# Strassen's scheme for the first feed-forward layer of the last six blocks

## The chip, the cores and the metric

The kernel runs on one core of a Trainium2 chip. The metric is the device time of one execution in microseconds (us), from launch to end, lower being better. A core has a matrix engine (TensorE, PE in the rows, with its weight loads listed apart as PEld), a vector engine (DVE), a scalar engine (ACT), a general engine (GpSimd, POOL), and a queue engine (SyncE, SP) that only issues DMAs. Each engine works through its own list of instructions in order and waits at semaphores for the others.

## The reference, cut to what matters

```python
def _moe_ref(x, w_ch1, w_ch2):
    X = np.fft.fft(x, axis=1)
    X = np.fft.fft(X, axis=2)
    u = x + np.real(X)
    mu = np.mean(u, axis=-1, keepdims=True)
    var = np.mean((u - mu) ** 2, axis=-1, keepdims=True)
    un = (u - mu) / np.sqrt(var + 1e-06)
    ch = np.maximum(un @ w_ch1, 0.0) @ w_ch2     # 512 -> 2048 -> 512
    return u + ch
```

`x` is the output of two attentions over 8 batches of 576 tokens (a pooled one and one in a band), 4608 tokens of 512 channels in all. Everything is float32.

## The kernel before

**Stages.** The first 330 us hold the attention, the Fourier mixing (as matrix products) and the decoding of the weights, which arrive as 64-bit numbers in quarters (class `Quarter`: fetch, size, clamp, join, high, low). The rest is the feed-forward part: nine blocks of 512 tokens (class `Block`, `NBLK` = 9, numbered 0 to 8).

**Three products for one.** The matrix engine multiplies in a rounded 32-bit format (`F32R`). To keep float32's precision each factor is held as a high part `h` and a low part `l`, and a product is taken as h·h + l·h + h·l. So w1 lies in SBUF as `wts[f, 1]` (two tiles of 128 x 4 x 128 per f, for the 16 groups f of 128 hidden channels), w2 as `wts[f, 2]`, and the transposed normalised tokens as `unT` (one such pair of 128 x 4 x 512 for even blocks and one for odd ones).

**One block.** For each f, `first` (line 958) issues 12 matmuls, 3 parts by 4 chunks of the 512 channels, each with 128 x 128 weights and 512 columns, into one PSUM bank `hps`. `high` (ACT, line 962) applies the ReLU into `hh`, `low` (DVE, line 966) makes `hl`, the rest. `second` (lines 976 to 978) issues 12 more matmuls of 512 columns that add the group's share into four accumulator banks `acc`. At the end of a block `finish` (DVE, line 982) adds the input `u`, `store` (line 986) writes it out. Meanwhile the next block's four tiles of 128 tokens are loaded (lines 900 to 906; the latter two kinds are adding DMAs issued by POOL), normalised (`stats`, `norm`), transposed on the matrix engine (`turn`, line 932: 4 matmuls into a bank `tpn`) and split (`turn_high` on ACT, `turn_low` on DVE). Four PSUM banks are `acc`; the other four are handed out by `bank`.

**Order of the work.** It is written out by hand: `at(fn, t=...)` files an event, and after the events placed by the table `TURNS` all others are issued in order of `t`. The unit `ITEM` (1.6) stands for 12 matmuls of 512 columns on the matrix engine, so an f takes 2 `ITEM` and a block 51.2 units. `second(f)` stands one `ITEM` after `first(f + 1)` has begun.

**Places in memory.** `raws` (four tiles of 128 x 512) and `joins` (four of 128 x 256) serve the decoding of the weights and are idle after it. `wts[f, 1]` is used by every block. Its tiles for f = 0 to 2 lie in the pool `res`, 3 and 4 in `pt`, 5 to 8 in `middle`, 9 to 15 in `more`.

Of the kernel before, what the change touches and what calls it, by code (L numbers as in the profile page):

```python
# [8 lines left out]
F32 = mybir.dt.float32  # L9
F32R = mybir.dt.float32r  # L10
# [3 lines left out]
ALU = mybir.AluOpType  # L14
# [10 lines left out]
ITEM = 1.6  # L25
# [220 lines left out]
def kernel(  # L246
# [13 lines left out]
    nc = tc.nc  # L260
    P = 128
# [4 lines left out]
    NCC = DM // P  # L266
    NF = DFF // P
# [107 lines left out]
    p1, plocal, pseq, pmix = (ExitStack() for _ in range(4))  # L375
# [3 lines left out]
    p2 = plocal.enter_context(tc.tile_pool(name="p2", bufs=2, side="right"))  # L379
# [36 lines left out]
    class Pooled:  # L416
# [258 lines left out]
    class Mix:  # L675
# [203 lines left out]
    out_rows = out.rearrange("b s c -> (b s) c")  # L879

    class Block:


        def __init__(self, n):
            self.n = n
            self.st, self.un, self.tp = {}, {}, {}
# [101 lines left out]
        def plan(self, t, f0, f1):  # L988

            for f in range(f0, f1):  # L990
                at(self.first, f, t=t)
# [42 lines left out]

    def close_d():
        pmix.close()
        weight_tiles(pool("more"), range(*CHUNKS[2:]))

    for close in (close_b, close_a, close_e, close_d):
        at(close)  # L1040
# [6 lines left out]
    t = 0.0  # L1047
    starts = {}
    for n, f0, f1 in [(0, 0, ROUND), (1, 0, ROUND), (0, ROUND, NF)] + [(n, ROUND * (n == 1), NF) for n in range(1, NBLK)]:
        starts[n] = t  # L1050
        t = blocks[n].plan(t, f0, f1)
        if f1 == NF and 0 < n < NBLK - 1:
            for i in range(TILES):
                for part in range(3):
                    at(blocks[n + 1].load, i, part, t=starts[n] + 6 + 0.5 * i + 2.5 * part)
                blocks[n + 1].prepare(i, starts[n] + 12 + i * (t - starts[n] - 18) / TILES)


    for x in quarters:
# [142 lines left out]
```

## Time and profile before

| | us |
|---|---|
| three runs | 1150.66, 1151.46, 1159.52 |
| their median | 1151.46 |
| the profiled execution | 1145.82 |
| its span, first to last instruction | 1144.0 |

The profiled execution was 5.6 us shorter than the median of the runs. Times in the rows are from its span's start. A matmul's busy time in the rows includes its way through the array and overlaps the next one's, so the rate of the matrix engine is read from the starts of successive rows, not from the mean of one.

### The profile page before, as it was taken

The page shows a single profiled execution, that of the slowest core. Times are in us where ns is not written, and L with a number is a line of the kernel's source. Part 1 is how long each engine was busy: PE and PEld are TensorE (multiplying, and loading weights), DVE is VectorE, ACT ScalarE, POOL GpSimd, SP SyncE. Part 2 cuts the span into 40 slices and gives each one's busy share as a digit, 9 for nine tenths or more (in the row PEclk, how much of TensorE's full clock was granted, in tenths as well). Part 3 has the DMA queues.
Part 4 walks back from the last instruction along what each step waited for, and adds up shares of the span by engine and source line. Part 5 has one row for each costly group of instructions (what it writes and reads, how often), then busy time and mean ns, then how long its engine had stood idle before and what let it go on. Part 6 is the DMA issues. An engine that isn't in the chain of part 4 may idle for free.

```text
span 1144.0 us, 20389 instructions
## 1 busy us (share of the span) xinstructions
PE 1108.0 (97%) x8172; PEld 935.8 (82%) x8172; DVE 545.4 (48%) x1226; ACT 358.4 (31%) x1050; POOL 293.5 (26%) x411
## 2 busy tenths in 40 slices
PE   7899999899889999999999999999999999999998
PEld 6788888889778788888888888888888888888886
DVE  4889999899878776322212222222222222222111
ACT  4777767767544443111111111111111111111110
POOL 2444545355574553203002002001101100200000
PEclk7999999999999999999999999999999999999999
DMA  8888777777685332506006005105103302400000
GB/s 257 269 257 252 215 240 247 234 217 181 181 188 161 109 123 93 110 1 148 1 1 147 1 1 129 19 1 121 27 1 95 53 1 71 77 1 37 1 1 37
DMA packets 57901, 123.07 MB, mean 108 GB/s; under 512 B 7280, under 2 KB 7408, under 8 KB 57552
## 3 DMA queue, kind: packets, MB, share of 16 engines
q1 hardware_dynamic: 44288, 92.23, 24.6%
q0 software_dynamic: 13520, 29.55, 14.7%
q8 instruction: 64, 1.05, 0.4%
q14 instruction: 29, 0.24, 0.1%
HBM read 89.88 MB, written 30.74 MB: 105 GB/s over the span
## 4 chain that ended last, share of the span: by engine, by line
PE 79%; DVE 10%; DMA 6%; issue 2%; SPq 1%; ACT 1%; POOL 0%; DVEq 0%; ACTq 0%; POOLq 0%
PE hps L958 34%; PE acc L976 11%; PE acc L978 11%; PE acc L977 11%; DMA vsum<-in_vg_dram 3%; PE y L744 2%; PE av L625 1%; PE avd L483 1%; PE sc L566 1%; PE tpn L932 1%; DVE sums L552 1%; DMA raw<-in_wq_dram 1%; PE mix L789 1%; DVE xeo L710 1%; DVE w L697 1%
## 5 line engine op out<-in xcount | busy, mean ns | idle before, releaser
L966 DVE SCALAR_TENSOR_TENSOR hl<-hps,hh 128x512 fp32r<-128x512 f32 x144 | 99.1, 690 | 456.3 <-ACT hh L962 456.3
L958 PE MATMUL hps<-unT,w1h 128*128 128x512 f32 x1152 | 309.9, 392 | 0.0
L962 ACT ACTIVATE hh<-hps 128x512 fp32r<-128x512 f32 x144 | 86.0, 598 | 539.2 <-PE hps L958 533.9
L958 PEld LDWEIGHTS hps<-unT,w1h 128*128 128x128 f32 x1152 | 215.5, 188 | 45.7
L976 PE MATMUL acc<-w2h,hh 128*128 128x512 f32 x576 | 227.3, 395 | 0.2 <-ACT hh L962 0.2
L978 PE MATMUL acc<-w2h,hl 128*128 128x512 f32 x576 | 225.5, 392 | 0.0
L977 PE MATMUL acc<-w2l,hh 128*128 128x512 f32 x576 | 225.4, 391 | 0.0
L958 PE MATMUL hps<-unT,w1l 128*128 128x512 f32 x576 | 155.2, 392 | 0.0
L978 PEld LDWEIGHTS acc<-w2h,hl 128*128 128x128 f32 x576 | 108.3, 188 | 24.0 <-DVE hl L966 0.4
L958 PEld LDWEIGHTS hps<-unT,w1l 128*128 128x128 f32 x576 | 108.3, 188 | 23.6
L976 PEld LDWEIGHTS acc<-w2h,hh 128*128 128x128 f32 x576 | 108.3, 188 | 23.4 <-ACT hh L962 0.6
L977 PEld LDWEIGHTS acc<-w2l,hh 128*128 128x128 f32 x576 | 108.3, 188 | 22.4
L917 POOL TENSOR_TENSOR rstd<-rstd,mhalf 128x1 f32<-128x1 f32 x36 | 19.9, 554 | 300.3 <-DVE rstd L916 299.1
L902 POOL DMA_DIRECT2D ut<-ux x40 | 35.5, 1002 | 206.7 <-DMA ut<-um 206.3
L584 ACT ACTIVATE sb<-sc,mx 128x64 f32<-128x64 f32 x320 | 69.8, 329 | 2.0 <-PE tpl L596 0.8
L941 DVE TENSOR_TENSOR unT<-tpn,unT 128x512 fp32r<-128x512 f32 x36 | 24.8, 688 | 55.4 <-ACT unT L938 55.4
L552 DVE TENSOR_REDUCE sums<-qkT 128x224 f32<-128x896 f32 (+4 forms) x48 | 44.4, 945 | 11.0 <-DMA qkT<-in_qk_dram 9.2
L566 PEld LDWEIGHTS sc<-qkT 64*64 64x64 f32 x1280 | 46.1, 141 | 3.8 <-DMA qkT<-in_qk_dram 0.6
L625 PE MATMUL av<-vaug,pT 64*64 64x65 f32 x1280 | 47.4, 224 | 1.3 <-DMA vaug<-in_vw_dram 0.7
L724 POOL TENSOR_TENSOR fl<-xeo,fh 128x512 fp32r<-128x512 f32 x32 | 42.0, 1334 | 21.8 <-ACT fh L721 16.3
L625 PEld LDWEIGHTS av<-vaug,pT 64*64 64x64 f32 x1280 | 42.2, 138 | 6.3 <-issue 2.9
L566 PE MATMUL sc<-qkT 64*64 64x64 f32 x1280 | 46.4, 225 | 0.1
(97 smaller groups left out, 1368.1 us busy)
## 6 DMA issues: line engine op xcount, KB each, us to landing
qkT<-in_qk_dram SPq DMA_DIRECT2D x40, 512.0 KB
raw<-in_wq_dram SPq DMA_DIRECT2D x64, 256.0 KB
vaug<-in_vw_dram SPq DMA_DIRECT2D x40, 260.0 KB
out_dram<-ut SPq DMA_DIRECT2D x36, 256.0 KB
um<-o SPq DMA_DIRECT2D x16, 512.0 KB
ut<-ux POOLq DMA_DIRECT2D x32, 256.0 KB, 5.1
ut<-ud POOLq DMA_DIRECT2D x32, 256.0 KB, 5.4
vsum<-in_vg_dram POOLq DMA_DIRECT2D x24, 292.5 KB, 6.7
```

The costliest lines, as they stand in the source:

```text
L552: nc.vector.tensor_reduce(out=to, in_=x[:, :, a - g0 : e - g0], axis=AX.X, op=ALU.add)
L566: nc.tensor.matmul(sc[r, a * W : (a + 1) * W], self.qkT[r, 0, a // 2, o : o + W], self.qkT[r, 1, a // 2, o : o + W], start=False, stop=Tru ...
L584: nc.scalar.activation(out=self.sb[:, a], in_=self.sc[:, a * W : (a + 1) * W], func=AF.Exp, scale=0.125, bias=self.mx[:, a : a + 1],)
L625: nc.tensor.matmul(av[r, a, :], pT[r, 4 * hh + a], va[r, 4 * hh + a, :], start=True, stop=True)
L724: nc.gpsimd.tensor_sub(out=self.fl[:, t], in0=self.x[t], in1=self.fh[:, t].bitcast(F32))
L902: nc.gpsimd.dma_start(out=to, in_=ux[b][k0 : k0 + m, :], accum_op=ALU.add)
L958: nc.tensor.matmul(hps, a[:, c, :], unT[:, x, c, :], start=(i == 0), stop=(i == len(mms) - 1))
L962: nc.scalar.activation(out=hh, in_=self.hps[f], func=AF.Relu)
L966: nc.vector.scalar_tensor_tensor(out=hl, in0=self.hps[f], scalar=0.0, in1=self.hh[f].bitcast(F32), op0=ALU.max, op1=ALU.subtract)
L976: nc.tensor.matmul(acc, hh, w2h, start=start, stop=False)
L977: nc.tensor.matmul(acc, hh, w2l, start=False, stop=False)
L978: nc.tensor.matmul(acc, hl, w2h, start=False, stop=stop)
```

## The change

For blocks 3 to 8 (`FAST` = 3) the product of the first layer is taken two groups f at a time: the 256 hidden channels of a pair j, by 512 channels, by 512 tokens. Each factor is cut into quarters (two halves of the channels by two groups f; two halves of the channels by two halves of 256 tokens), and Strassen's scheme in Winograd's form gives the four quarters of the result from seven products of quarters (p1 = a11·b11, then s2·t2 added onto it; p2 = a12·b21; p3 = s4·b22; p5 = s1·t1; p7 = s3·t3, then a22·t4 added onto it). A product of quarters is 6 matmuls (3 parts by 2 chunks) with 128 x 128 weights and 256 columns. So a pair takes 42 matmuls of 256 columns for 24 of 512. `second` is as it was.

What goes with it:

- `Differences`, once for each of the 8 pairs, in the last part of block 1 and the first of block 2: joins high and low part of w1 again (`rejoin`, DVE), forms t1 to t4 (`differ`, POOL, 4 subtractions), splits them (`high` on ACT, `low` on POOL) and writes the seven quarters and differences to DRAM (`keep`, 14 DMAs of 128 KB a pair on SP).
- `stream`: each pair in each fast block loads its seven pieces of 256 KB back from DRAM on SP, into tiles of `wts[4..10, 1]`, which are no longer needed as such; two sets, by the parity of j.
- For each coming fast block `turn_copy` (ACT) copies the transposed tile, `add_up` (POOL) forms the sums s1 to s4 of quarters, `sum_high` (ACT) and `sum_low` (POOL) split them into `wts[0..3, 1]` (odd blocks) or `wts[12..15, 1]` (even blocks).
- In a fast pair `save` (ACT) copies p1 twice out of PSUM, and `combine` (DVE, six times) adds the products up into two tiles `rows`, from which `high` and `low` now read instead of from PSUM.
- The three banks of a pair are `ab` (p1, p3), `cd` (p2, p5) and `ef` (p7).

```diff
+    STEPS = ("b11", "b21", "t1"), ("t2", "t3"), ("t4", "b22")
...
+        def rejoin(self):
+            for k in range(2):
+                h, l = wts[2 * self.n + k, 1]
+                whole = raws[k].rearrange("p (c f) -> p c f", c=NCC)
+                nc.vector.tensor_add(out=whole, in0=h.bitcast(F32), in1=l.bitcast(F32))
+
+        def differ(self):
...
+            for out, a, b in ((t1, b12, b11), (t2, b22, t1), (t3, b22, b12), (t4, b21, t2)):
+                nc.gpsimd.tensor_sub(out=out, in0=a, in1=b)
...
+        def plan(self, t):
+            at(self.rejoin, t=t)
+            at(self.differ, t=t + 0.5)
+            for i, x in enumerate(parts[3:]):
+                at(self.high, x, t=t + 2.5 + 0.1 * i)
+                at(self.low, x, t=t + 2.55 + 0.1 * i)
+                at(self.keep, x, t=t + 3 + 0.1 * i)
+            for x in parts[:3]:
+                at(self.keep, x, t=t)
...
+            mms = [(y, z, c) for y, z in ((0, 0), (1, 0), (0, 1)) for c in range(2)]
+            for i, (y, z, c) in enumerate(mms):
+                nc.tensor.matmul(
+                    into, w[:, y, c, :], both[z][:, c, :], start=(start and i == 0), stop=(i == len(mms) - 1), skip_group_check=True
+                )
+
+        def open(self, j):
+            ps = [bank("ab"), bank("cd"), bank("ef")]
...
+            self.product(j, self.ps["p1"], "a11", "b11")
+            self.product(j, self.ps["p2"], "a12", "b21")
+            self.product(j, self.ps["p5"], "s1", "t1")
+
+        def more(self, j):
+            self.product(j, self.ps["p1"], "s2", "t2", start=False)
+            self.product(j, self.ps["p7"], "s3", "t3")
+
+        def close(self, j):
+            self.product(j, self.ps["p7"], "a22", "t4", start=False)
+            self.product(j, self.ps["p3"], "s4", "b22")
...
+        def fast_pair(self, j, t):
+
+            f = 2 * j
+            for g, d in enumerate((0.85, 1.35, 2.65)):
+                at(self.stream, j, g, t=t + (d - 8) * ITEM if j > 1 else t + (d - 5) * ITEM)
+            at(self.open, j, t=t)
+            at(self.save, 0, "p1", t=t + 0.5 * ITEM)
+            at(self.more, j, t=t + 0.8 * ITEM)
+            at(self.combine, 11, 0, "p2", t=t + 0.85 * ITEM)
+            at(self.save, 1, "p1", t=t + 1.1 * ITEM)
+            at(self.combine, 2, 1, "p5", t=t + 1.15 * ITEM)
+            at(self.combine, 22, 2, "p7", t=t + 1.3 * ITEM)
+            at(self.close, j, t=t + 2 * ITEM)
+            at(self.combine, 21, 1, "p7", t=t + 2.3 * ITEM)
+            at(self.combine, 12, 2, "p3", t=t + 2.6 * ITEM)
+            for g, d in ((f, 2.45), (f + 1, 3.1)):
+                at(self.hidden, g, t=t + d * ITEM)
+                at(self.high, g, t=t + d * ITEM)
+                at(self.low, g, t=t + (d + 0.05) * ITEM)
+            at(self.second, f, f == 0, False, t=t + 5 * ITEM)
+            at(self.second, f + 1, False, f + 1 == NF - 1, t=t + 7 * ITEM)
...
+            if n + 1 == FAST:
+                for j in range(NF // 2):
+                    Differences(j).plan(starts[n] - 18 + 4 * j)
```

On the matrix engine one f of block 3 stood so before, `first` and the beginning of the other group's `second` (the name after the comma is the weights, the one before it what moves past them):

```order
L958 MATMUL hps<-unT_6051,w1h_6364 128x512 x4
L958 MATMUL hps<-unT_6051,w1l_6365 128x512 x4
L958 MATMUL hps<-unT_6051,w1h_6364 128x512 x4
L976 MATMUL acc<-w2h_6362,hh 128x512 [waits Activation_49]
L977 MATMUL acc<-w2l_6363,hh 128x512
L978 MATMUL acc<-w2h_6362,hl 128x512 [waits DVE_49]
```

In the changed program pair 1 of block 3 begins on the matrix engine with five products (`open` and `more`); names w1h and w1l with numbers are now the places of streamed pieces, to the right of the comma, or of sums, to its left:

```order
L1066 MATMUL ab<-unT_6107,w1l_6117 128x256 x6
L1066 MATMUL cd<-unT_6107,w1h_6120 128x256 x6
L1066 MATMUL cd<-w1h_140,w1h_6412 128x256 x4
L1066 MATMUL cd<-w1l_141,w1h_6412 128x256 x2
L1066 MATMUL ab<-w1h_144,w1l_6413 128x256 x4
L1066 MATMUL ab<-w1l_145,w1l_6413 128x256 x2
L1066 MATMUL ef<-w1h_148,w1h_6416 128x256 x4
L1066 MATMUL ef<-w1l_149,w1h_6416 128x256 x2
L1143 MATMUL acc<-w2h_142,hh 128x512
L1144 MATMUL acc<-w2l_143,hh 128x512
L1145 MATMUL acc<-w2h_142,hl 128x512
```

After the 12 rows of that `second` its `close` follows, on the matrix engine, here with the semaphores that it waits for:

```order
L1066 MATMUL ef<-unT_6107,w1l_6417 128x256 [waits DMAHW1_49,DVE_49]
L1066 MATMUL ef<-unT_6107,w1l_6417 128x256 x5
L1066 MATMUL ab<-w1h_5924,w1l_6121 128x256 [waits DMAHW2_49,Activation_49]
L1066 MATMUL ab<-w1h_5924,w1l_6121 128x256 x3
L1066 MATMUL ab<-w1l_5925,w1l_6121 128x256 x2
```

Where 12 long matmuls with one bank stood, 30 short ones in three banks stand in a row, and then 12 more; each product waits for the DMA of its weights, and those that add onto a bank also for ACT or DVE, which read it.

On ACT the ReLUs of block 2 stood alone before but for a cast of a transposed tile between them:

```order
L962 ACTIVATE hh<-hps 128x512 x2
L938 CAST unT_6051<-tpn 128x4x128
L962 ACTIVATE hh<-hps 128x512 x3
L938 CAST unT_6051<-tpn 128x4x128
L962 ACTIVATE hh<-hps 128x512 x2
```

Now the casts of the differences t1 to t4 (`raw` and `wt` in these rows) stand between the ReLUs on ACT, from block 1's last part on, and wait for POOL:

```order
L923 CAST raw<-raw 128x256 [waits DMAHW7_49,Activation_49,Pool_49]
L923 CAST raw<-raw 128x256 [waits DMAHW1_49,Activation_49,Pool_49]
L923 CAST wt<-wt 128x256 [waits DMAHW3_49,Activation_49,Pool_49]
L923 CAST wt<-wt 128x256 [waits DMAHW5_49,Activation_49,Pool_49]
L1129 ACTIVATE hh<-hps 128x512 [waits DVE_49,PE_49]
L923 CAST raw<-raw 128x256 [waits DMAHW5_49,Activation_49,Pool_49]
L923 CAST raw<-raw 128x256 [waits DMAHW7_49,Activation_49,Pool_49]
L923 CAST wt<-wt 128x256 [waits DMAHW1_49,Activation_49,Pool_49]
L923 CAST wt<-wt 128x256 [waits DMAHW3_49,Activation_49,Pool_49]
```

A ReLU that stood behind the matrix engine alone now stands behind four casts, which stand behind POOL's subtractions and the DMAs that empty their places.

## Rows read from the trace of the kernel before

**Rows 1.** The page: span, busy share, granted clock by slices

```profile
span 1144.0 us, 20389 instructions
PE 1108.0 (97%) x8172; PEld 935.8 (82%) x8172; DVE 545.4 (48%) x1226; ACT 358.4 (31%) x1050; POOL 293.5 (26%) x411
...
PEclk7999999999999999999999999999999999999999
```

**Rows 2.** The page: the chain that ended last, by engine

```profile
PE 79%; DVE 10%; DMA 6%; issue 2%; SPq 1%; ACT 1%; POOL 0%; DVEq 0%; ACTq 0%; POOLq 0%
```

**Rows 3.** Same chain, in order of time: start us, us, what

```profile
601.18 2.81 PE hps L958 x12
...
634.91 2.72 PE hps L958 x12
...
690.80 2.81 PE hps L958 x12
...
1049.32 2.81 PE hps L958 x12
```

**Rows 4.** PE timeline, a transposed tile: start us, us, engine line op

```profile
640.20 0.60 PE L932 MATMUL tpn<-ident,un 128*128 128x128 f32 x4
640.55 1.18 PE L958 MATMUL hps<-unT,w1h 128*128 128x512 f32 x4
```

**Rows 5.** PE timeline, twelve matmuls of 256 columns in a row

```profile
355.96 0.40 PE L789 MATMUL mix<-chanm,yh 128*68 128x256 f32 x2
...
356.67 0.40 PE L789 MATMUL mix<-chanm,yh 128*128 128x256 f32 x2
356.90 0.28 PE L789 MATMUL mix<-chanm,yl 128*128 128x256 f32 x1
...
357.37 0.40 PE L976 MATMUL acc<-w2h,hh 128*128 128x512 f32 x1
```

**Rows 6.** Line 958's weight loads and its two waits by the load's sequencer

```profile
L958 PEld LDWEIGHTS hps<-unT,w1h x1152: 186/188/193, 329.2 to 1133.6; 128*128 128x128 f32 x192
...
L958 PEldq EVENT_SEMAPHORE  x2: 51/51/51, 327.4 to 349.7; - x2
```

**Rows 7.** Groups, whole span: name, shapes, count, busy us, mean ns, idle before

```profile
L966 DVE SCALAR_TENSOR_TENSOR hl<-hps,hh 128x512 fp32r<-128x512 f32 x144 | 99.1, 690 | 456.3 <-ACT hh L962 456.3
L962 ACT ACTIVATE hh<-hps 128x512 fp32r<-128x512 f32 x144 | 86.0, 598 | 539.2 <-PE hps L958 533.9 <-PE acc L977 5.3
L982 DVE TENSOR_TENSOR ut<-acc,ut 128x512 f32<-128x512 f32 x44 | 27.9, 683 | 4.2 <-PE acc L978 4.2
L371 POOL TENSOR_TENSOR w2l<-wt,w2h 128x256 fp32r<-128x256 f32 x32 | 24.8, 782 | 26.1 <-ACT w2h L367 25.4 <-DVE xeo L710 0.6
L643 DVE TENSOR_TENSOR xb<-av,rs 128x256 f32<-128x256 f32 (+1 forms) x48 | 18.9, 421 | 0.9
L751 ACT CAST yh<-y 128x290 fp32r<-128x290 f32 x32 | 12.7, 411 | 19.2 <-PE y L744 18.9
```

**Rows 8.** ACT timeline, one ReLU in block 1

```profile
468.80 0.60 ACT L962 ACTIVATE hh<-hps 128x512 fp32r<-128x512 f32 x1 [4.84 <-PE hps L958]
```

**Rows 9.** PE timeline, the end of the next group's `first` after it

```profile
473.13 1.07 PE L958 MATMUL hps<-unT,w1h 128*128 128x512 f32 x4
474.04 0.60 PE L932 MATMUL tpn<-ident,un 128*128 128x128 f32 x4
```

**Rows 10.** The page: SP's DMA queue, packets, MB, share of 16 engines

```profile
q1 hardware_dynamic: 44288, 92.23, 24.6%
```

**Rows 11.** Line 906, adding DMAs by POOL: issue to landing

```profile
DMA to landing us min/median/max: 3.0/5.1/8.1
```

**Rows 12.** Windows, block 3's loads in block 2: us; busy by engine; clock, DMA share, GB/s

```profile
522.00:533.00 11.00, 11.00 (x48) 8.87 (x48) 1.75 (x3) 1.20 (x2) 6.84 (x8) 1.00 1.00 191
```

**Rows 13.** SP's weight fetches of 256 KB: ns to issue one

```profile
L327 SPq DMA_DIRECT2D raw<-in_wq_dram x64: 327/331/1108, 57.6 to 439.8; - x64
```

More of the change, by code (lines that the diff above doesn't have):

```diff
@@ L238 @@
 TILES = 4
+FAST = 3
 WARM_UP = 40
@@ L286 @@
     um = [dram.tile([2, KEPT, DM], F32, name=f"um{b}") for b in range(B)]
+    parts = "b11", "b21", "b22", "t1", "t2", "t3", "t4"
+    uw = [{x: dram.tile([P, 2, HN], F32, name=f"u{x}{j}") for x in parts} for j in range(NF // 2)]
     res = ctx.enter_context(tc.tile_pool(name="res", bufs=1))
@@ L879, with spare, streamed, __init__ @@
     out_rows = out.rearrange("b s c -> (b s) c")
+    def spare(n):
+        return wts[n // 2, 1][n % 2].rearrange("p c f -> p (c f)")
+    def streamed(j):
+        return {x: spare(2 * TILES + len(parts) * (j % 2) + k) for k, x in enumerate(parts)}
+    STEPS = ("b11", "b21", "t1"), ("t2", "t3"), ("t4", "b22")
+    class Differences:
+        def __init__(self, n):
+            self.n = n
+            self.w = wts, 2 * n
+            self.t = {}
+        def blocks(self, x):
+            f, c = 2 * self.n + int(x[2]) - 1, 2 * (int(x[1]) - 1)
+            return [t[:, c : c + 2, :].rearrange("p c f -> p (c f)") for t in wts[f, 1]]
+        def rejoin(self):
[4 more added lines that the diff above has]
+        def differ(self):
+            b11, b21, b12, b22 = (raws[k][:, i * HN : (i + 1) * HN] for k in range(2) for i in range(2))
+            places = [(r[:, :HN], r[:, HN:]) for r in raws[2:4]] + [
+                (joins[i].bitcast(F32), joins[i + 1].bitcast(F32)) for i in (0, 2)
+            ]
+            self.t = dict(zip(("t1", "t2", "t3", "t4"), places))
+            t1, t2, t3, t4 = (l for h, l in places)
+            for out, a, b in ((t1, b12, b11), (t2, b22, t1), (t3, b22, b12), (t4, b21, t2)):
+                nc.gpsimd.tensor_sub(out=out, in0=a, in1=b)
+        def high(self, x):
+            h, l = self.t[x]
+            nc.scalar.copy(out=h.bitcast(F32R), in_=l)
+        def low(self, x):
+            h, l = self.t[x]
+            nc.gpsimd.tensor_sub(out=l.bitcast(F32R), in0=l, in1=h)
+        def keep(self, x):
+            pair = self.t[x] if x in self.t else [t.bitcast(F32) for t in self.blocks(x)]
+            for i, t in enumerate(pair):
+                nc.sync.dma_start(out=uw[self.n][x][:, i, :], in_=t)
+        def plan(self, t):
[7 more added lines that the diff above has]
+                at(self.keep, x, t=t)
     class Block:
@@ L885, in __init__ @@
             self.n = n
+            self.c, self.ps = {}, {}
             self.st, self.un, self.tp = {}, {}, {}
@@ L949, in prepare, with turn_copy, sums, side @@
                 at(fn, i, t=t + d)
+        def turn_copy(self, i):
+            nc.scalar.copy(out=raws[i], in_=self.tp[i])
+        def sums(self):
+            return [[spare(2 * TILES * k + 2 * x + part) for part in range(2)] for k, x in ((self.side, y) for y in range(4))]
+        @property
+        def side(self):
+            return 0 if self.n % 2 else 3
+        def add_up(self, i):
+            a11, a12 = (raws[i][:, k * HN : (k + 1) * HN].rearrange("p (c n) -> p c n", c=2) for k in range(2))
+            a21, a22 = (raws[i + 2][:, k * HN : (k + 1) * HN].rearrange("p (c n) -> p c n", c=2) for k in range(2))
+            for out, a, b, op in (
+                (a22, a21, a22, ALU.add),
+                (a21, a11, a21, ALU.subtract),
+                (a11, a22, a11, ALU.subtract),
+                (a12, a12, a11, ALU.subtract),
+            ):
+                nc.gpsimd.tensor_tensor(out=out, in0=a, in1=b, op=op)
@@ new lines, in sum_of, with sum_high, sum_low @@
+        def sum_of(self, k, i):
+            whole = raws[i if k % 2 else i + 2][:, (0 if k in (1, 2) else HN) :][:, :HN]
+            at_i = slice(i * P, (i + 1) * P)
+            parts = [y.rearrange("p (c n) -> p c n", c=2)[:, :, at_i] for y in self.sums()[k]]
+            return whole.rearrange("p (c n) -> p c n", c=2), *parts
+        def sum_high(self, k, i):
+            s, h, l = self.sum_of(k, i)
+            nc.scalar.copy(out=h, in_=s)
+        def sum_low(self, k, i):
+            s, h, l = self.sum_of(k, i)
+            nc.gpsimd.tensor_sub(out=l, in0=s, in1=h.bitcast(F32))
@@ new lines, in stream, with product @@
+        def stream(self, j, g):
+            for x in STEPS[g]:
+                to = streamed(j)[x]
+                nc.sync.dma_start(out=to.bitcast(F32), in_=uw[j][x].rearrange("p x f -> p (x f)"))
+        def product(self, j, into, a, x, start=True):
+            w = streamed(j)[x].rearrange("p (x c f) -> p x c f", x=2, c=2)
+            if a[0] == "a":
+                r, k = (int(y) - 1 for y in a[1:])
+                both = [unTs[self.n % 2][:, y, 2 * k : 2 * k + 2, r * HN : (r + 1) * HN] for y in range(2)]
+            else:
+                both = [y.rearrange("p (c n) -> p c n", c=2) for y in self.sums()[int(a[1]) - 1]]
+            mms = [(y, z, c) for y, z in ((0, 0), (1, 0), (0, 1)) for c in range(2)]
[3 more added lines that the diff above has]
+                )
@@ new lines, in close, with save, combine, hidden @@
+        def close(self, j):
+            self.product(j, self.ps["p7"], "a22", "t4", start=False)
+            self.product(j, self.ps["p3"], "s4", "b22")
+        def save(self, k, x):
+            nc.scalar.copy(out=joins[k].bitcast(F32), in_=self.ps[x])
+        def combine(self, to, a, x):
+            place = lambda k: joins[k].bitcast(F32) if k < 3 else rows[k % 10 - 1][:, (k // 10 - 1) * HN : k // 10 * HN]
+            nc.vector.tensor_add(out=place(to), in0=place(a), in1=self.ps[x])
+        def hidden(self, f):
+            self.hps[f] = rows[f % 2]
@@ L990, in plan @@
             for f in range(f0, f1):
+                if self.n >= FAST:
+                    if f % 2 == 0:
+                        self.fast_pair(f // 2, t)
+                    t += 2 * ITEM
+                    continue
                 at(self.first, f, t=t)
@@ L995, in plan @@
                 t += 2 * ITEM
+            late = 2 * ITEM if self.n >= FAST else 0
             for i in range(TILES):
-                at(self.finish, i, t=t + (1.3 + 0.25 * i) * ITEM)
+                at(self.finish, i, t=t + late + (1.3 + 0.25 * i) * ITEM)
                 if f1 == NF:
-                    at(self.store, i, t=t + (1.6 + 0.25 * i) * ITEM)
+                    at(self.store, i, t=t + late + (1.6 + 0.25 * i) * ITEM)
             return t
     blocks = [Block(n) for n in range(NBLK)]
-    pacc = [None]
+    pacc, rows = [None], []
     for b in range(B):
@@ L1036, in close_d @@
         pmix.close()
-        weight_tiles(pool("more"), range(*CHUNKS[2:]))
+        more = pool("more")
+        weight_tiles(more, range(*CHUNKS[2:]))
+        rows.extend(more.tile([P, TILES * P], F32, name=f"row{i}") for i in range(2))
     for close in (close_b, close_a, close_e, close_d):
@@ L1055 @@
                     at(blocks[n + 1].load, i, part, t=starts[n] + 6 + 0.5 * i + 2.5 * part)
-                blocks[n + 1].prepare(i, starts[n] + 12 + i * (t - starts[n] - 18) / TILES)
+                x, t0 = blocks[n + 1], starts[n]
+                if n + 1 < FAST:
+                    x.prepare(i, t0 + 12 + i * (t - t0 - 18) / TILES)
+                    continue
+                for d, fn in ((0, x.stats), (2.5, x.norm), (5, x.turn), (5.5, x.turn_copy), (5.9, x.turn_high), (6.2, x.turn_low)):
+                    at(fn, i, t=t0 + 22 + 3 * i + d)
+                if i > 1:
+                    at(x.add_up, i - 2, t=t0 + 29 + 3 * i)
+            if n + 1 >= FAST:
+                for k in range(4):
+                    for i in range(2):
+                        d = (6 + k // 2) * 4 * ITEM + (1.35 + 0.22 * (2 * (k % 2) + i)) * ITEM
+                        at(x.sum_high, k, i, t=t0 + d)
+                        at(x.sum_low, k, i, t=t0 + d + 0.4 * ITEM)
+            if n + 1 == FAST:
+                for j in range(NF // 2):
+                    Differences(j).plan(starts[n] - 18 + 4 * j)
     for x in quarters:
```

1 line of the change is left out of this document (added).

## The prediction

> **What bounds the kernel now.** I read the page first: the matrix engine is busy 97% of the span, and its clock is fully granted from the second slice on, so at 2.4 GHz of its two levels [rows 1]; the chain that ended last is 79% matrix engine [rows 2]. A busy matrix engine need not be at its peak, so I went on to that chain in order of time. Blocks 3 and 4 begin at 601.18 and 690.80, so a block takes 89.62 us [rows 3]. It holds 384 matmuls of 512 columns (16 groups f by 12 + 12) and four transposed tiles of 0.35 us (640.20 to 640.55 [rows 4]): (89.62 - 1.40) / 384 = 229.7 ns a matmul, with no gap left. ACT's ReLU idles for the matrix engine 533.9 us, DVE's `hl` for the ReLU 456.3 us [rows 7]: both have time. So a feed-forward block is matmuls times their spacing, and only fewer or shorter matmuls shorten it.
>
> Twelve matmuls of the first group of a block take 2.81 us, of later ones 2.72. That is so in block 8 at 1049.32 too, when there is no later block to load [rows 3]: it goes with the place of the weights, not with the DMAs.
>
> **The change, part by part.**
>
> *Matmuls.* Removed: 6 blocks x 192 = 1152 of 512 columns, at 229.7 ns 264.6 us. Added: 6 x 8 pairs x 42 = 2016 of 256 columns. The trace has such matmuls in the mixing stage: twelve in a row from 355.96 to 357.37, 117.5 ns each, and the last six of them, with weights of the full width, 0.70 us, 117 ns [rows 5]. I take 118: 237.9 us, so 26.7 us less. Bounds: half of a good long one, 2.72 / 24 = 113 ns, makes it 36.8 less; the other end is the weight load's own 188 ns [rows 6], which makes it 114.4 more. I stay at the row of the same shape.
>
> *Operands.* In odd blocks s1 to s3 lie in the tiles of f = 0 to 2, the groups of the 2.81. That is 7.5 ns a long matmul; for a short one I take half, 3.75 ns x 18 matmuls x 8 pairs x 3 blocks = 1.6 us more (0 to 3.2).
>
> *Waits inside a pair.* By the new order a pair is `open` 18 x 0.118 = 2.12 us, `more` 1.42, one `second` 2.72, `close` 1.42, one `second` 2.72: 10.4 us, where two f took 11.0. ACT can copy p1 from 0.7 us on and needs 0.41, like the cast of 290 columns [rows 7]; `more` adds onto p1 at 2.12. The second copy is due at about 3.3, then three `combine`, 0.42 each by the DVE row of that size [rows 7], end near 4.6; `close` wants them at 6.26. In pair 1 of each block a `low` (until about 1.4) and four `finish` of 0.68 [rows 7] stand before them in DVE's list: they end near 5.4, still 0.8 early. So I cost them at nothing; the cover is the first `second`, and each us beyond it would come 48 times, or 6 times for pair 1. `finish` then frees the accumulators in time for the next `second`, at 3.5.
>
> Four of a pair's seven products wait for two semaphores, which takes a wait of its own on the engine: 51 ns each where the trace has one [rows 6]. I take zero, since the sequencer gets ahead of an array that needs 118 ns a matmul; fully exposed it is 4 x 48 x 51 ns = 9.8 us.
>
> *Other engines in a pair.* DVE 6 x 0.42 + 2 x 0.69 = 3.9 us, ACT 2 x 0.41 + 2 x 0.60 = 2.0 us, of 10.4; POOL 16 operations of 0.78 us a block, 12.5 us of 83 [rows 7]. Hidden.
>
> *The stream.* 7 x 256 KB = 1.84 MB a pair. SP's queue moved 92.23 MB in 24.6% of 16 engines' 1144 us, 328 GB/s [rows 10], so 5.6 us of 10.4; issuing costs SP 7 x 0.33 = 2.3 us [rows 13]. The pieces are asked for 5 to 7 `ITEM` ahead of `open`, over 13 us. Hidden; priced as a rival below.
>
> *The differences, in blocks 1 and 2.* They come every 4 units, 4 / 51.2 x 89.62 = 7.0 us. Per pair POOL works 8 x 0.78 = 6.3 us [rows 7], the DMAs 1.84 MB / 328 = 5.6 us, SP 14 x 0.33 = 4.6 us: each just fits. But block 3's loads fall into the same stretch: the DMA engines are full from 522 to 533 as it is, and POOL spends 6.84 us there on issuing [rows 12], with landings of 5.1 us between [rows 11]. I expect the last two groups to be some 8 us late. ACT's casts wait for them with the ReLU behind. The ReLU has cover: one ends at 469.40, and the `second` that needs it cannot start before 474.04, 4.6 us later [rows 8, 9]. So the matrix engine loses about 3 us. Bounds: 0, if POOL keeps its pace; and if every group waits for a landing, 6.3 + 5.1 = 11.4 for 7.0, seven times 4.4 less the cover, 26 us.
>
> *Ends.* The turns are as many as before. At the end of block 8 three `second` follow the last `close`, and its `hh` and `hl` are made under the first of them: nothing.
>
> **The sum.** -26.7 + 1.6 + 3.0 = -22.1 us. The profiled execution took 1145.8 us (span 1144.0 [rows 1] and 1.8 around it), so the same execution would take 1123.7. The runs shown have a median of 1151.5, 5.6 above it; I put the same difference on the median: 1129.4 us.
>
> **Rivals.**
>
> *A, the weight loads pace the short matmuls (slower).* A load is busy for 188 ns [rows 6]. Under a long matmul (230 ns) it is covered; short ones at 118 ns need the loads to overlap one another, and there are 30 in a row now, where the trace shows twelve [rows 5]. If they overlap only half, the spacing is (118 + 188) / 2 = 153 ns: 308.4 us for 264.6, +43.8 + 4.6, 1199.9 us. It decides from 264.6 / 2016 = 131 ns on. Against it: the last six of the twelve are no slower than the first. The Trainium skill ("TensorE: Matmul & The Clock Gate", Back-to-back issue gap) gives for sustained pairs of load and matmul 81 ns at 128 columns and 131 at 512; a straight line between them puts 256 at 98 (my estimate), and a pair would go from 24 x 131 = 3.1 to 42 x 98 = 4.1 us, 47 us more in all. The trace does not agree: 229.7 and 117.5 ns, a ratio of 0.51 where the page's is 0.75. Chance 0.06.
>
> *B, the differences hold up the ReLUs throughout (no change).* The upper bound above: 1151.5 - 26.7 + 1.6 + 26 = 1152.4 us. For it: DMAs and POOL both near full. Against it: the cover of 4.6 us, and writes of one pair can land under the next pair's `rejoin`. Chance 0.07.
>
> *C, the waits at the heads of the products show.* Four of 51 ns a pair cost 9.8 us, all seven 17.1: 1139.2 to 1146.5 us. Against it: `hh` and `hl` are waited for in every `second` now, and nothing is seen of it in the 229.7. Chance 0.09.
>
> *D, the stream paces the pairs (slower).* At the 191 GB/s of a full queue with adding DMAs in it [rows 12], a block's eight pairs take 8 x 9.6 = 77 us, and its own 4.2 MB of loads and stores 22: 99 for 89.6, +56 in all, 1208 us. It decides below (14.7 + 4.2 MB) / 89.6 = 211 GB/s. Against it: the 328 GB/s of SP's own queue [rows 10]. Chance 0.04.
>
> **How the numbers follow.** My forecast has 0.74, with an own range of 1118 (spacing 114 ns, no lateness) to 1142 (122 ns and 5 us more of lateness). With C and part of B the range is 1118 to 1148; A, D and the rest of B are left out. A measurement of this kernel can tell about 1% from no change, 11.5 us. Faster by more than that, below 1140: nearly all of the forecast and the mild end of C, 0.73. Within 1%: the rest of C, the forecast's slow end and nearly all of B, 0.16. Slower: A, D and the worst of B, 0.11.
>
> **What would show it.** Right: in blocks 3 to 8 runs of matmuls of 256 columns at 116 to 120 ns, pairs of 10.4 us, blocks of about 85 us, no idle time of the matrix engine ahead of `close`; in block 2 a few gaps before `second`, ended by ACT, near 530 to 545 us. Wrong: a spacing above 125 ns in the long runs (A), gaps at each product's head (C) or ended by DMA (D), a block 2 that is 10 us or more longer than 89.6 (B).

## The result, and the profile after

The changed kernel takes 1139.89 us (median of 4 runs, 1136.72 to 1142.15), the kernel before beside it 1151.2: a ratio of 0.988, 95% interval 0.984 to 0.992. In a second set it was 1138.48 against 1150.44, 0.9885 (0.985 to 0.992). The forecast was 1129.4, with a range of 1118 to 1148: faster, as said, by 11.3 us where 22.1 were said. The profiled execution of the changed kernel took 1138.89 us.

From the page of the changed kernel, what answers to [rows 1] and [rows 2]:

```profile
span 1137.1 us, 24102 instructions
...
PE 1096.8 (96%) x9036; PEld 967.3 (85%) x9036; DVE 652.0 (57%) x1482; ACT 435.4 (38%) x1250; POOL 413.7 (36%) x571
...
PE 69%; DMA 15%; DVE 6%; SPq 3%; issue 2%; POOL 2%; ACT 2%; ACTq 0%; POOLq 0%; DVEq 0%
```

The matrix engine's share hardly fell, and it has 864 matmuls more (2016 short for 1152 long). What happened is seen by blocks. The trace in windows from block to block (the first matmul of one to that of the next; blocks 2 to 8; the number ahead of PEclk is POOL's):

```profile
core 0: us, PE busy (x) PEld busy (x) DVE busy (x) ACT busy (x) POOL busy (x), PEclk, DMA share, GB/s
515.90:612.07 96.17, 91.81 (x401) 74.67 (x400) 26.89 (x46) 21.47 (x48) 45.70 (x61) 0.98 0.55 158
612.07:695.99 83.92, 83.52 (x533) 75.80 (x532) 36.92 (x79) 21.96 (x47) 20.84 (x28) 1.00 0.75 226
695.99:783.20 87.21, 86.55 (x545) 78.16 (x544) 37.56 (x80) 22.59 (x48) 22.53 (x30) 1.00 0.72 217
783.20:869.31 86.11, 86.11 (x545) 78.01 (x544) 37.56 (x80) 22.59 (x48) 20.84 (x28) 1.00 0.72 220
869.31:956.50 87.19, 86.52 (x545) 78.15 (x544) 37.65 (x80) 22.70 (x48) 22.45 (x30) 1.00 0.71 218
956.50:1043.32 86.82, 86.36 (x545) 78.06 (x544) 37.66 (x80) 22.71 (x48) 20.85 (x28) 1.00 0.72 218
1043.32:1133.22 89.90, 89.90 (x553) 80.63 (x551) 32.07 (x64) 16.70 (x33) 0.00 (x0) 1.00 0.44 143
```

The same before, for block 8:

```profile
1049.14:1139.68 90.54, 90.54 (x397) 74.24 (x395) 15.46 (x23) 9.57 (x16) 0.00 (x0) 1.00 0.04 14
```

Before, each of blocks 2 to 7 took 89.63 us [rows 3] and block 8, up to the end of its last matmul, 90.5. Now blocks 3 to 8 take 83.9, 87.2, 86.1, 87.2, 86.8 and 89.9, together 521.2 for 538.7: 17.5 us less, where the forecast had 25.1. (Block 3 is short and block 8 long because two `second` of each block now run in the next, where it was one: 12 matmuls of 2.75 us change sides.) Block 2, still computed in the old way, takes 6.5 us more, where the forecast had 3. That makes -11.0, and the medians say -11.3. The two profiled spans differ by 6.9 only, since block 2 began at 515.9 instead of 511.4. In nine traces of kernels whose code up to there is the same, but for the first differences in block 1, it began between 509.5 and 521.7. Block 1's last eleven groups, where those differences lie, took 64.5 to 65.5 us in all nine: nearly all of that spread belongs to code that the change doesn't touch.

**Block 2.** The matrix engine behind its one gap, in order of time:

```profile
550.94 0.50 PE L1143 MATMUL acc<-w2h,hh 128*128 128x512 f32 x1 [4.36 <-ACT hh L1129]
...
552.09 0.63 PE L1143 MATMUL acc<-w2h,hh 128*128 128x512 f32 x1
552.51 0.63 PE L1144 MATMUL acc<-w2l,hh 128*128 128x512 f32 x1
```

and two windows, the gap and what follows:

```profile
546.20:550.90 4.70, 0.39 (x2) 0.00 (x0) 0.00 (x0) 1.43 (x5) 2.39 (x4) 1.00 1.10 284
550.90:555.40 4.50, 4.46 (x11) 3.26 (x12) 1.29 (x2) 0.47 (x1) 4.50 (x8) 0.62 1.02 176
```

A `second` waits 4.36 us for a ReLU. Behind it the granted clock is 0.62 for 4.5 us: matmuls of 512 columns start 0.43 us apart, the lower of the two levels, where they start 0.23 apart otherwise. Some ten at 0.43 cost another 2.1 us. With the 4.4 that is the whole 6.5. Who was late stands in POOL's list:

```profile
532.24 1.55 POOL L919 TENSOR_TENSOR raw<-raw 128x256 f32<-128x256 f32 x2 [2.84 <-DMA ut<-raw]
...
536.21 0.89 POOL L966 DMA_DIRECT2D ut<-ux  x1 [1.02 <-DMA ut<-um]
...
541.61 2.68 POOL L966 DMA_DIRECT2D ut<-ux  x3 [0.87 <-DMA ut<-um]
544.00 1.87 POOL L919 TENSOR_TENSOR raw<-raw 128x256 f32<-128x256 f32 x2
547.79 0.72 POOL L919 TENSOR_TENSOR wt<-raw 128x256 f32<-128x256 f32 x1 [1.91 <-DMA ut<-wt]
```

and in ACT's:

```profile
549.99 0.40 ACT L923 CAST wt<-wt 128x256 fp32r<-128x256 f32 x1 [1.04 <-POOL wt L919]
550.30 1.08 ACT L1129 ACTIVATE hh<-hps 128x512 fp32r<-128x512 f32 x2
```

The last group's subtractions (L919, `differ`) follow those of the group before by 11.8 us (532.24 to 544.00), not by 7.0: between them POOL issues the adding loads of block 3's tokens (L966) and waits for the load ahead of them (`um`). Inside the last group it then waits for writes of the group before (`ut<-wt`), 1.91 us ahead of the third subtraction. ACT's casts wait behind POOL, the ReLU behind the last cast.

**Blocks 3 to 8.** The second to fifth product of pair 1 in block 4, in order of time; each row is part of a product of six:

```profile
707.22 0.88 PE L1066 MATMUL cd<-unT,w1h 128*128 128x256 f32 x6
707.94 0.64 PE L1066 MATMUL cd<-w1h,w1h 128*128 128x256 f32 x4
...
708.66 0.64 PE L1066 MATMUL ab<-w1h,w1l 128*128 128x256 f32 x4
...
709.38 0.64 PE L1066 MATMUL ef<-w1h,w1h 128*128 128x256 f32 x4
```

The products begin at 707.22, 707.94, 708.66 and 709.38: 0.72 us each, so 120 ns a matmul, and nothing added at a product's head. What the engine waited for in blocks 3 to 8:

```profile
PE cd L1066 <- DMA w1l<-ut: 0.7, 2, 0.5
PE ef L1066 <- DVE st L977: 0.5, 1, 0.5
PE ab L1066 <- DMA w1h<-ut: 0.4, 1, 0.4
PE ab L1066 <- ACT wt L1086: 0.4, 1, 0.4
```

(total, times, longest, in us): few, and small. The chain that ended last [rows 2] has more DMA now, 15% for 6%, but that is no sign that transfers pace the blocks: it follows such a stall back through the whole way of the piece that ended it. One step of it, in block 7, start us, us, what:

```profile
986.27 14.43 DMA w1l<-ut
```

This piece was 14.4 us on its way, and the matrix engine stood 0.5 us for it.

### The profile page after: what moved, and what is told of

Its sections match the earlier page's. It is cut to its first block, busy times and chain, and to the rows that moved or that the text cites. A ratio compares the mean times of both kernels' runs of the same rounds, so it can differ in the third digit from the quotient of the medians.

```text
span 1137.1 us, 24102 instructions
## 1 busy us (share of the span) xinstructions
PE 1096.8 (96%) x9036; PEld 967.3 (85%) x9036; DVE 652.0 (57%) x1482; ACT 435.4 (38%) x1250; POOL 413.7 (36%) x571
## 4 chain that ended last, share of the span: by engine, by line
PE 69%; DMA 15%; DVE 6%; SPq 3%; issue 2%; POOL 2%; ACT 2%; ACTq 0%; POOLq 0%; DVEq 0%
PE acc L1143 9%; PE acc L1145 9%; PE acc L1144 9%; PE hps L1125 8%; PE ab L1066 7%; PE ef L1066 5%; PE cd L1066 5%; PE y L747 3%; DMA vsum<-in_vg_dram 3%; DMA ux<-xa 2%; DMA raw<-in_wq_dram 2%; PE av L628 2%; PE sc L569 2%; PE avd L486 2%; DMA w1h<-ut 2%
## 5 line engine op out<-in xcount | busy, mean ns | idle before, releaser
L1129 ACT ACTIVATE hh<-row 128x512 fp32r<-128x512 f32 x96 | 60.7, 632 | 283.2 <-DVE row L1091 191.1
L1133 DVE SCALAR_TENSOR_TENSOR hl<-row,hh 128x512 fp32r<-128x512 f32 x96 | 68.8, 716 | 119.3 <-ACT hh L1129 119.3
L1091 DVE TENSOR_TENSOR row<-wt,ef 128x256 f32<-128x256 f32 x96 | 40.3, 420 | 110.0 <-PE ef L1066 105.6
L1125 PE MATMUL hps<-unT,w1h 128*128 128x512 f32 x384 | 101.9, 391 | 0.0
L966 POOL DMA_DIRECT2D ut<-ux x40 | 35.9, 965 | 155.0 <-DMA ut<-um 149.4
L1133 DVE SCALAR_TENSOR_TENSOR hl<-hps,hh 128x512 fp32r<-128x512 f32 x48 | 32.6, 687 | 93.4 <-ACT hh L1129 93.4
L1125 PEld LDWEIGHTS hps<-unT,w1h 128*128 128x128 f32 x384 | 71.8, 188 | 15.2
L1086 ACT COPY wt<-ab 128x256 f32<-128x256 f32 x96 | 35.7, 372 | 93.7 <-PE ab L1066 93.7
L1129 ACT ACTIVATE hh<-hps 128x512 fp32r<-128x512 f32 x48 | 28.4, 596 | 89.2 <-PE hps L1125 83.0
L1050 POOL TENSOR_TENSOR w1l<-raw,w1h 128x256 fp32r<-128x256 f32 x48 | 33.9, 738 | 62.3 <-ACT w1h L1046 62.3
L1125 PE MATMUL hps<-unT,w1l 128*128 128x512 f32 x192 | 51.6, 391 | 0.0
```

Source lines behind the costliest of these rows:

```text
L1091: nc.vector.tensor_add(out=place(to), in0=place(a), in1=self.ps[x])
L1129: nc.scalar.activation(out=hh, in_=self.hps[f], func=AF.Relu)
L1133: nc.vector.scalar_tensor_tensor(out=hl, in0=self.hps[f], scalar=0.0, in1=self.hh[f].bitcast(F32), op0=ALU.max, op1=ALU.subtract)
```

## The experiments

The theory after this reading: the gain per block is smaller because a short matmul costs more than half a long one, by a fixed part; and block 2 loses because the last differences and block 3's loads meet. The rivals: the stream, or the preparation's own pace.

**The preparation alone.**

```
-FAST = 3
+FAST = 9
+PREPARED = 3
-            if n + 1 == FAST:
+            if n + 1 == PREPARED:
```

> The differences of the weights' quarters are made and written out in blocks 1 and 2 as in the changed kernel, but blocks 3 to 8 run their first layer in the old way, 12 matmuls of 512 columns a group; nothing of the preparation is read. It prices the preparation by itself. Theory (the preparation holds up block 2 by the 6.5 us that the changed kernel's block 2 is longer, of which 4.4 us is one gap before a `second`): 1151.2 + 6.5 = about 1157.7 us, block 2 about 96 us long with a gap ended by ACT near its first third, blocks 3 to 8 at 89.6 us. Rival 1 (the forecast's term, 3 us): 1154. Rival 2 (the preparation is free, and block 2 of the changed kernel is longer for the sums and casts of block 3 that lie in it, which this kernel leaves out): 1151, block 2 at 89.6 us.

Measured: 1167.42 us, ratio 1.0146 (1.010 to 1.019). None of the three: block 2 takes 107.7 us, blocks 3 to 7 89.6 to 89.8. All that the matrix engine waited for from block 2 on, then DVE's list:

```profile
PE tpn L997 <- DVE un L989: 15.3, 1, 15.3
```

```profile
537.94 0.69 DVE L1134 SCALAR_TENSOR_TENSOR hl<-hps,hh 128x512 fp32r<-128x512 f32 x1
555.10 0.70 DVE L978 BATCH_NORM_STATS2 st<-ut 128x6 f32<-128x512 f32 x1 [16.48 <-DMA ut<-ud]
```

Without fast blocks, block 3's statistics go back to their old place, 12 units into block 2, and the differences hold up the loads that they need: DVE stands 16.5 us before `ud` has landed. So the run doesn't price the preparation by itself, but it shows that the two do meet: the loads come late, and the last group of differences, 11.7 us behind the one before it, does too.

**The stream in block 3 alone.**

```
             for g, d in enumerate((0.85, 1.35, 2.65)):
-                at(self.stream, ...)
+                if self.n == FAST:
+                    at(self.stream, ...)
```

> Only block 3 streams the quarters and differences; blocks 4 to 8 multiply whatever of them is left in the places (so their first layer is computed with the weights of other groups), with the same 42 matmuls a pair. It takes 5 x 14.7 MB of transfers away. Theory (a matmul has a fixed part: 120 ns for 256 columns and 227 ns for 512 are columns plus 32 steps at 2.4 GHz): the spacing stays at 120 ns and `second` at 227 to 231 ns; only the few stalls ended by a DMA go, about 1.5 us in all: 1138. Rival 1 (the transfers into the same memory cost 2 ns a matmul): the spacing in blocks 4 to 8 falls to 118 ns and `second` back to 229.6 or less: 5 x (336 x 2 + 192 x 1.5) ns = 4.8 us and the stalls, 1133. Rival 2 (the stream paces the pairs): pairs fall well below 10.5 us.

Measured: 1139.47 us, ratio 0.991 (0.988 to 0.995): nothing gained in the total. (Its profiled execution had a gap of 5.9 us in block 2, the longest of the three seen, and a block 2 of 98.0 us.) Blocks 4 and 5 in windows, then all that the matrix engine waited for from block 2 on:

```profile
703.67:789.73 86.06, 86.06 (x545) 78.05 (x544) 37.69 (x80) 22.71 (x48) 22.55 (x30) 1.00 0.23 50
789.73:875.84 86.11, 86.11 (x546) 78.02 (x544) 37.62 (x80) 22.72 (x48) 20.87 (x28) 1.00 0.23 50
```

```profile
PE acc L1144 <- ACT hh L1130: 5.9, 1, 5.9
PE ab L1066 <- ACT wt L1086: 0.4, 1, 0.4
```

With the DMA share down from 0.72 to 0.23, a block without a stall still takes 86.1 us, as block 5 did with the stream, and the median spacing stays at 120 ns (336 matmuls in 40.28 us). The stream costs its stalls, 0 to 1.1 us a block and 3.0 us in blocks 4 to 7 together, not the rate. Rivals 1 and 2 fall. The matmuls of `second` stay at a mean of 231 ns, where they took 229.6 before: these 1.4 ns are not the stream's either.

**256 columns without Strassen.**

```
-            for i, (a, x, c) in enumerate(mms):
-                nc.tensor.matmul(hps, a[:, c, :], unT[:, x, c, :], ...)
+            for k in (slice(0, HN), slice(HN, DM)):
+                for i, (a, x, c) in enumerate(mms):
+                    nc.tensor.matmul(hps[:, k], a[:, c, :], unT[:, x, c, k], ...)
```

> The kernel before, with each of the 144 groups of the first layer computed as twelve matmuls of the first 256 columns and twelve of the other 256, instead of twelve of 512: the same sums, no differences, no stream, no sums of operands. It measures the 256-column matmul in long runs by itself. Theory (fixed part of 32 steps a matmul): 120 ns each, a group 24 x 120 = 2.88 us where it was 2.76, so 144 x 0.12 = +18 us: 1169. Rival 1 (118 ns is their own rate, and the stream made it 120): +144 x (24 x 0.118 - 2.756) = +11 us: 1162. Rival 2 (half the columns, half the time): no change, 1151.

Measured: 1175.01 us, ratio 1.020 (1.014 to 1.027). A group in block 7, in order of time:

```profile
1063.30 0.64 PE L959 MATMUL hps<-unT,w1l 128*128 128x256 f32 x4
1063.78 1.12 PE L959 MATMUL hps<-unT,w1h 128*128 128x256 f32 x8
```

Four matmuls take 0.48 us: 120 ns, with no stream, no sums and no differences. Blocks 2 to 7 take 91.7 us for 89.63. The theory's 120 ns stands. The cuts account for 12.5 us in blocks 2 to 7, 2.3 in block 8 and 3.9 in the 32 groups ahead (768 matmuls at a mean of 119.4 ns for 384 at 228.6), 19 us as expected. The rest of the 23.5 is put down to the spread ahead of block 2, which began at 529.3 here; this is not shown further.

**Other widths.**

```
+            cuts = {4: (0, 384, 512), 6: (0, 128, 256, 384, 512), 8: (0, 256, 512)}.get(self.n, (0, 512))
+            for lo, hi in zip(cuts, cuts[1:]):
+                k = slice(lo, hi)
...
```

> The kernel before, with the first layer's matmuls cut in other widths in three blocks: 384 + 128 columns in block 4, four times 128 in block 6, two times 256 in block 8; the other blocks as they were. Theory (a matmul takes its columns and 32 steps more, at 2.4 GHz): 173 ns for 384, 67 ns for 128, 120 ns for 256; a block grows by 2.1 us with one cut (measured with halves) and by three times that, 6.3 us, with three: blocks 4, 6 and 8 at 91.7, 95.9 and 92.6 us. Rival 1 (weight loads set a floor somewhere below 120 ns): 128 columns take clearly more than 67 ns, 90 to 190, and block 6 is over 100 us. Rival 2 (the fixed part belongs to 256 columns only): 384 + 128 columns take the 227 ns of 512.

Measured: 1206.68 us in one run; blocks 4, 6 and 8 took 100.9, 131.9 and 92.8 us. In block 4, four of 384 and four of 128 columns to a row:

```profile
780.47 0.61 PE L961 MATMUL hps<-unT,w1l 128*128 128x128 f32 x4
780.91 0.61 PE L961 MATMUL hps<-unT,w1h 128*128 128x128 f32 x4
...
784.16 0.87 PE L961 MATMUL hps<-unT,w1h 128*128 128x384 f32 x4
784.87 0.86 PE L961 MATMUL hps<-unT,w1l 128*128 128x384 f32 x4
```

The median spacing is 227 ns for 512 columns, 174 for 384, 120 for 256 and 111 for 128. At 2.4 GHz the first three are 545, 418 and 288 steps: columns and 32 to 34 more. So the fixed part of 13 to 14 ns holds from 512 down to 256, and rival 2 falls. At 128 the time stops falling: 111 ns, not 67. Rival 1 is right that there is a floor, and 256 columns lie 9 ns above it. That it is the weight load's is not shown: no run here changed the load itself, and the loads' busy times in the rows overlap one another at a spacing of 120 and of 111. The Trainium skill ("TensorE: Matmul & The Clock Gate", LDWEIGHTS (loading the stationary operand)) puts a load at its number of columns over 1.2 GHz, so one of 128 columns at 107 ns (my estimate from it), however many rows it has. The 111 ns would agree with such a floor; the load's busy time in the rows, 186 to 193 ns, is longer than that figure.

**Block 3's loads later.**

```
-                    at(blocks[n + 1].load, i, part, t=starts[n] + 6 + 0.5 * i + 2.5 * part)
+                    at(blocks[n + 1].load, i, part, t=starts[n] + (11 if n == 2 else 6) + 0.5 * i + 2.5 * part)
```

> The changed kernel, with the loads of block 3's tokens in block 2 asked for 5 units of the order (8.8 us) later, so that they come after the last differences rather than among them. Theory (the last group of differences was late because POOL and the DMA queue were held by these loads): the gap of 4.4 us in block 2 goes and most of the 6.5 us with it, block 2 near 90 us, 1139.9 - 5.5 = about 1134.5. Rival 1 (the preparation is late of itself, since POOL, DMA and SP can't keep a group in 7.0 us): the gap stays, 1140. Rival 2 (the loads now come late for block 3's statistics, and the sums for block 3 with them): block 3's first products wait, 1142 or more.

Measured: 1132.25 us, ratio 0.985 (0.979 to 0.991). Block 2 takes 90.65 us, with no gap ahead of a `second`; one of 0.8 us ahead of a turn is left. The same again, with more runs:

> The kernel with block 3's loads 5 units later, again, to tell it from the changed kernel with more runs (1138.5 to 1139.9 us so far). Theory (it saves block 2's 5.5 us, whatever the first 510 us do): 1133.5, ratio 0.984 or 0.985 to the kernel before; block 1's last eleven groups at 64.7 us, block 2 at 90.6. Rival (its 1132.3 was chance, and the loss moves elsewhere as it did with the earlier differences): 1138 to 1140.

Measured: 1132.38 us, ratio 0.9835 (0.980 to 0.987). Block 2 in a window, and POOL's list at the last two groups:

```profile
512.15:601.78 89.63, 89.63 (x401) 73.65 (x400) 28.34 (x46) 21.94 (x48) 47.27 (x62) 1.00 0.57 169
```

```profile
528.49 1.56 POOL L919 TENSOR_TENSOR raw<-raw 128x256 f32<-128x256 f32 x2 [2.26 <-DMA ut<-raw]
...
535.09 1.56 POOL L919 TENSOR_TENSOR raw<-raw 128x256 f32<-128x256 f32 x2
...
542.95 2.59 POOL L966 DMA_DIRECT2D ut<-ux  x3 [1.97 <-DMA ut<-um]
```

The last group's subtractions now follow the group before by 6.6 us (528.49 to 535.09), the loads come behind, and block 2 takes the 89.63 us of before with the whole preparation in it. So the last group keeps its 7.0 us when no load stands before it, and the collision was the cost. Whether POOL's issuing or the full DMA engines make up more of it was not told apart. This kernel beats both, by 6 to 8 us the changed one.

**The changed kernel again, and the differences earlier.**

> The changed kernel as it is, beside the two that follow. Its first 512 us are the code of the kernel before, and block 2 began between 509.5 and 521.7 us in the runs of the same code so far. Theory (that spread is chance, the losses are in block 2): a time near 1139.9 us, block 2 at about 96 us whatever the time at which it begins, blocks 4 to 7 at 86 to 87 us. Rival (the lateness in block 2 is chance too): block 2 anywhere between 90 and 98 us.

Measured: 1138.48 us; block 2 takes 97.5 us with a gap of 4.9 us, from 514.3 on. The rival falls: with a gap of 4.4, 4.9 and 5.9 us in three traces, the loss is there each time.

```
-                    Differences(j).plan(starts[n] - 18 + 4 * j)
+                    Differences(j).plan(starts[n] - 25 + 4 * j)
```

> The changed kernel, with all eight groups of differences placed 7 units (12.3 us) earlier, so that the last is planned before block 3's loads, which stay where they were. Theory (the two collide: the last differences wait behind loads on POOL and the DMA queues): no gap of more than 1 us ahead of a `second`, no stretch at the lower clock in block 2, block 2 at 90 us, and -5.5 to -6.5 us against the changed kernel: about 1134. Rival 1 (a group takes more than its 7.0 us whatever lies beside it): the last groups still end 8 us or more behind their place; a cover of 12.3 us hides it, and the differences' own subtractions stand more than 7.0 us apart all along. Rival 2 (earlier means into block 1, where differences meet block 2's statistics): a gap in block 1 instead, 1139.

Measured: 1139.75 us, ratio 0.989 (0.985 to 0.993). Block 2 takes 89.63 us without a gap, yet nothing is won: rival 2. Block 1's last eleven groups take 71.0 us where the changed kernel takes 64.7. What the matrix engine waited for there:

```profile
PE tpn L996 <- DVE un L988: 3.4, 3, 2.5
PE acc L1145 <- DVE hl L1133: 0.5, 1, 0.5
```

A turn waits for block 2's `norm`, which waits for `rstd`, an operation of POOL behind the differences; the gap of 2.5 us, at 491.5, is again followed by six matmuls 0.43 us apart.

**Statistics later in every block.** On top of the earlier differences:

```
-                for d, fn in ((0, x.stats), (2.5, x.norm), (5, x.turn), ...
+                for d, fn in ((2, x.stats), (3.2, x.norm), (5, x.turn), ...
```

> The same, and the statistics of the next block's tokens placed 2 units (3.5 us) later in every block, the turns left where they are: on DVE they waited 2.8 to 4.2 us for the last of the token loads, with the `combine` of the pair behind them, and the matrix engine then lost 0.5 to 1.0 us ahead of a product in `ef`. Theory: the gaps ended by DVE in blocks 4 and 5 go, blocks 4 to 7 come to 86.1 us each as they are without the stream, and the whole to about 1132.5. Rival (the stalls are the stream's own, a weight's piece that lands late): the gaps stay, ended by DMA, no difference from the kernel with the earlier differences alone.

Measured: 1139.55 us, ratio 0.988 (0.984 to 0.993). The waits of blocks 3 to 8:

```profile
PE tpn L996 <- DVE un L988: 0.9, 5, 0.2
PE ef L1066 <- DMA w1l<-ut: 0.8, 1, 0.8
PE ab L1066 <- DMA w1h<-ut: 0.6, 2, 0.3
PE ef L1066 <- DMA w1h<-ut: 0.5, 1, 0.5
PE ef L1066 <- DVE st L977: 0.4, 1, 0.4
PE ab L1066 <- ACT wt L1086: 0.4, 1, 0.4
```

The rival: most of what waited for DVE's statistics now waits for a streamed piece or for a `norm`, and blocks 4 to 7 take 87.1 to 88.0 us. All stalls but 0.4 us in block 3 go with the stream, as its absence showed above; that they come where it shares the DMA engines with the loads fits the changed kernel's block 4 (DMA share 1.08 about its stall at 742 us) and was not tried by itself. Block 1's last eleven groups take 71.4 us here, with gaps of 2.5 and 2.2 us, but behind these the granted clock stays at 1.00. The first of them on the matrix engine, then a window from its end on:

```profile
492.33 0.66 PE L996 MATMUL tpn<-ident,un 128*128 128x128 f32 x4 [2.52 <-DVE un L988]
```

```profile
492.30:495.00 2.70, 2.67 (x14) 2.30 (x15) 2.70 (x4) 0.59 (x1) 2.70 (x3) 1.00 0.74 250
```

So one gap of 2.5 us was followed by the lower clock and another was not.

**Both at once, in block 2 alone.** Loads 4 units later, `stats` to `add_up` 1 unit later for n == 2:

> Block 3's loads 4 units later, and its statistics, turns and sums 1 unit later in block 2 alone. Theory (what was left there was one gap of 0.8 us ahead of a turn, since the statistics waited for the later loads): block 2 at 89.7 us, 1 us below the kernel with the loads 5 units later, too little for the times to tell. Rival (loads 4 units later meet the last differences again): a gap ahead of a `second` and a block 2 over 91 us.

Measured: 1135.07 us, ratio 0.985 (0.981 to 0.988), block 2 at 90.2 us. Within the spread of the kernel with the later loads; not a step further.

## Why the prediction was right, and where its sum was off

The direction and the range were right, the size was about half of what was said. All terms but the operand place came out worse than priced, so little was hidden by errors that cancel; the time stays in the range since its slow end (122 ns a matmul and 5 us more of lateness) left room for about as much. That the median falls below 1140, the forecast's own line for a clear gain, by 0.1 us in one set and 1.5 in the other is close to luck.

*Direction, and what bounds the kernel:* right. The blocks are matmuls times spacing, before and after; blocks 3 to 8 have 2 us of idle in 521.

*Matmuls, -26.7 at 118 ns:* mis-sized. A block without stalls has 336 in 40.28 us, 119.9 ns; six blocks 241.7 us, so -22.9. I took the spacing from one run of twelve in the mixing stage [rows 5]; runs of thirty, and the cut groups of the kernel before, give 120. That row was no outlier: the mixing stage's 256-column matmuls have a median of 118 ns, and why they are 2 ns faster was not tried. What the forecast did not see is that long and short matmuls carry the same fixed 13 ns; its 118 held 11 of them unnamed. Seven products for eight is 7/8 in columns, and (42 x 120) / (24 x 227) = 0.925 in time.

*Operand place, +1.6:* 0. Odd and even blocks without a stall both have 40.28 us (in the run that streams in block 3 alone); in odd blocks the matmuls of s1 to s3 come 116 to 125 ns apart in a pattern whose mean is 120.

*Waits inside a pair, 0:* right in the rule, 3.6 us in all (245.3 us in six blocks for 241.7), of which 3.0 go when the stream goes; 2.2 of it are the idle times, the rest the slower first matmuls behind them. Rival C, the heads of the products, falls by the rows above: 0.72 us from head to head.

*`second`:* not in the sum, +1.7 us (231.0 ns for 229.6). Behind a run of short ones its first five matmuls take 229 to 235 ns in the mean, where they took 228 to 229; the cut groups of the kernel before show the same. Why was not tried.

*The stream:* hidden, as said, but for these stalls. The forecast had the pieces asked for over 13 us ahead; the one above took 14.4. Rival D falls: with and without it, a block without a stall takes 86.1 us.

*Differences in blocks 1 and 2, +3:* 6.5. The mechanism (the last group late, ACT's casts ahead of the ReLU, 4.4 us left after its cover) and the sign were as forecast, the place (546 us for 530 to 545) nearly; the step that failed priced the gap at its own length, 3 us for 4.4, when the lower clock behind it added half as much again. Rival B, all groups late, falls: the last two came 9.5 and 11.8 us after the one before, but only the last held up a ReLU. By an estimate from block 2's start and 1.75 us a unit they stood 5 and 10 us behind their place, where the forecast had 8 for both.

*Rival A:* the spacing needed, 131 ns or more, did not come: the loads, busy 186 to 193 ns each, overlap one another at 120. A floor exists below that, 111 ns at 128 columns; whether loads set it is open.

Together: -22.9 + 3.6 + 1.7 + 6.5 = -11.1 us, for -22.1. Two thirds of the miss are in blocks 3 to 8, one third in block 2.

## What to carry to other kernels

Price a scheme that trades fewer products for narrower ones by the measured spacing at both widths, not by columns: each matmul brought 13 ns of its own here, and that took 40% of Strassen's eighth. When one-off preparation is put beside a busy stage, look for the periodic work of the other stages that shares its queue (here the next block's loads) and keep them apart; moved forward, it met another stage's work, moved behind it met none. And a gap of the matrix engine can cost more than its length: here those of 4.4 us and more all had slow matmuls behind them, those of about 2.5 us once and once not.

## What the runs showed of the hardware

- The fixed part of a matmul appears at the full clock: 227, 174 and 120 ns for 512, 384 and 256 columns. At the lower level 512 columns take 427 ns (block 2 of the changed kernel, behind the gap), which is 512 steps of 1.2 GHz and nothing more. The Trainium skill ("TensorE: Matmul & The Clock Gate", Wait — 56ns, not 53.3ns?) also has a fixed part that shows only at the full clock, but of 2.5 ns; here it is 13 to 14, in this kernel's type and with a load for every matmul.
- From 256 to 128 columns the spacing falls by 9 ns only, to 111. The turns of the kernel before had shown it: their matmuls of 128 columns start 108 ns apart (median of the second to fourth).
- After idle times of 4.4 to 15.3 us (four traces) the clock was granted at its lower level, for 4.5 us of matmuls behind the one of 4.4. Behind one of 2.50 us it was granted at that level for 3.4 us, behind others of 2.52 and 2.21 us it stayed at 1.00, as it did behind those of up to 1.0 us in blocks 3 to 7.
